# Attention before a mixture of experts: exponentials turned by a product with the diagonal of their inverse sums

## The chip, the core and the metric

The kernel runs on one core of one Trainium2 chip. The metric is the device time of one execution, in microseconds (us). Three runs of the kernel before gave 2071.26, 2071.85 and 2072.37 us; their median is 2071.85.

## What is computed

First comes attention for 4 batches, 8 heads, 768 positions and 64 channels a head, with a mask that keeps the first 8 keys and the last 96 positions. Then a mixture of 8 experts runs on its output of 3072 rows, with weights from eight rounds of alternating normalisation. The attention's share that matters here:

```python
scores = scale * np.matmul(q, k.transpose(0, 1, 3, 2))
...
scores = scores - np.max(scores, axis=-1, keepdims=True)
a = np.exp(scores)
a = a / (np.sum(a, axis=-1, keepdims=True) + 1e-09)
return np.matmul(a, v).astype(np.float32)
```

The division by the sum of a row is what the change moves. A row's sum belongs to a query.

## The kernel before, in words

The class `Banded` does the attention in 32 units of work: a batch, a half of the sequence (3 tiles of 128 queries) and a pair of heads. A unit has three groups, one for each tile of queries, and a group holds both heads. Groups are numbered through as t, from 0 to 95. Because of the mask a tile of queries meets at most 256 keys, so a group has four blocks of 128 keys by 128 queries; the first group of a unit in the first half has two. All units together have 352 blocks.

A group goes through these steps:
- `prepare` (line 309): TensorE turns q and k (tiles `tp`), and ScalarE and VectorE split them into a high and a low part (`qh`, `ql`, `kh`, `kl`).
- `scores` (line 329): three products for each head into PSUM (`s_ps`), for two groups at a time.
- `softmax` (line 352): VectorE adds the bias and finds the row's maximum (line 368, tiles `p_sb` and `mx`); ScalarE takes the exponential and its row sum (line 373, `sm`).
- Behind the third group of a unit, the six sums get EPS (lines 383 and 385), VectorE takes reciprocals (line 386), and a copy spreads each over 64 columns (line 389, tile `inv`).
- `turn` (line 397): TensorE transposes the blocks of exponentials against the identity (line 403, recorded at line 131; from `p_sb` to `t_ps`), and ScalarE or VectorE copies the result to SBUF (line 406, `pT`).
- `invert` (line 494): TensorE transposes the three spread inverses of a unit (`r_ps`), and VectorE copies them back over `inv` (line 500).
- `values` (line 409) and `flush` (line 479): the products of values and turned exponentials (`o_ps`), with channels on the partitions. The two heads write the two halves of the 128 partitions. Then `o_ps` is multiplied by `inv` (line 489), and split into two parts for the experts (lines 490 and 491, tiles `x`).

The order on TensorE is written out by hand. A round does two units, and the tables `FIRST_ROUND` to `ROUND` (lines 58 to 61) say in which order. S is scores and softmax of two groups, T turns two groups, O is `flush`, P is `prepare`, R is `invert` of one unit, and F is filling work for the experts. From the third round on, the rounds start with S, O, S, S. `InOrder` (line 121) keeps TensorE in program order; the order on ScalarE, VectorE and GpSimd is the scheduler's. PSUM tiles of the attention come from one pool of six. `CHUNK` is 2, the number of groups in a step S or T; `P` is 128, `D` is 64, `UT` is 3.

GpSimd works on the experts' weights and inputs meanwhile. Behind the attention the experts fill the rest of the span; there TensorE is busy nearly without a break.

Of the kernel before, what the change touches and what calls it, by code (L numbers as in the profile page):

```python
# [54 lines left out]
BIAS = ((None, (32, 256), (128, 352)), ((0, 384), (32, 256), (128, 352)))  # L55


FIRST_ROUND = (("S", 0), ("O", 0), ("T", 0), ("F", 4), ("P", 0), ("S", 1), ("T", 1), ("F", 4), ("R", 0), ("S", 2), ("R", 1), ("T", 2), ("F", 4), ("P", 1))
SECOND_ROUND = (("S", 0), ("O", 0), ("T", 0), ("F", 4), ("P", 0), ("S", 1), ("T", 1), ("F", 4), ("R", 0), ("R", 1), ("S", 2), ("T", 2), ("F", 4), ("P", 1))
THIRD_ROUND = (("S", 0), ("O", 0), ("S", 1), ("S", 2), ("F", 2), ("T", 0), ("F", 1), ("F", 1), ("T", 1), ("F", 1), ("F", 1), ("P", 0), ("F", 1), ("F", 1), ("T", 2), ("P", 1), ("F", 1), ("R", 0), ("R", 1), ("F", 1), ("F", 1), ("F", 1))  # L60
ROUND = (("S", 0), ("O", 0), ("S", 1), ("S", 2), ("F", 2), ("T", 0), ("F", 1), ("F", 1), ("T", 1), ("F", 1), ("F", 1), ("P", 0), ("F", 1), ("F", 1), ("T", 2), ("F", 1), ("R", 0), ("R", 1), ("F", 1), ("P", 1), ("F", 1), ("F", 1))


class Ordered:
# [69 lines left out]
class Banded:  # L134
# [15 lines left out]
    def __init__(self, tc, q, k, v, early, n_bias):  # L150

        self.tc, self.nc = tc, tc.nc
        self.q, self.k, self.v = q, k, v
        self.H, self.D = q.shape[1], q.shape[3]
        assert n_bias == self.H * self.BIAS1
        self.bias1, rest = early, early[:, n_bias:]
        self.early_q = rest[:, 0:self.Q]
        self.early_k = rest[:, self.Q:self.Q + self.K]
        self.early_v = rest[:, self.Q + self.K:self.Q + self.K + self.V]
        self.d0 = rest[:, self.Q + self.K + self.V:]  # L160
        self.d1 = early[:, n_bias - self.BIAS1:n_bias + self.BIAS1]

        self.early_own = early[:, 5 * self.BIAS1:5 * self.BIAS1 + 2 * P]
        self.second_q = early[:, 4 * self.BIAS1:4 * self.BIAS1 + self.Q]
        self.warm = early[:, 6 * self.BIAS1:6 * self.BIAS1 + 2 * P].bitcast(mybir.dt.bfloat16)
        self.work = [(b, half, g) for b in range(q.shape[0]) for half in range(2) for g in range(self.H // 2)]
        self.pending, self.done, self.begun = [], 0, []
        self.sums, self.inv, self.outs = {}, {}, {}

        self.queue = Ordered(tc, self.nc.sync)  # L170
        self.pe = InOrder(tc)
        self.qs, self.ks, self.vs, self.ready, self.scored = {}, {}, {}, {}, {}
# [179 lines left out]
    def softmax(self, t, s_list):  # L352


        nc, D = self.nc, self.D
        n, group = divmod(t, len(GROUPS))
        _, half, g = self.work[n]
        p_sb = self.wrk.tile([P, 2, 2, P], F32, name="p_sb")
        mx = self.wrk.tile([P, 2], F32, name="mx", bufs=4)
        if group == 0:  # L360
            self.sums[n] = self.wrk.tile([P, UT, 2], F32, name="sm", bufs=4)
        sm = self.sums[n]
        views = []
        for u, (j, i) in enumerate(GROUPS[group]):
            h = 2 * g + j
            pv = p_sb[:, u, 0:len(KEYS[half][i])]
            views.append(pv)
            nc.vector.tensor_tensor_reduce(out=pv, in0=s_list[u], in1=self.bias(h, half, i), scale=-(D ** -0.5), scalar=3.0e38,  # L368
                                           op0=ALU.add, op1=ALU.min, accum_out=mx[:, u:u + 1])
        def exponentials(scalar, us=(0, 1)):  # L370
            for u in us:
                j, i = GROUPS[group][u]
                scalar.activation(out=views[u], in_=views[u], func=AF.Exp, bias=mx[:, u:u + 1], scale=-1.0,  # L373
                                  accum_out=sm[:, i, j:j + 1])

        if t < CHUNK:
            self.begun.append(exponentials)
            return p_sb
        exponentials(nc.scalar)
        if group == len(GROUPS) - 1:  # L380
            begins = n < self.H // 2
            if begins:
                nc.vector.tensor_scalar(out=sm, in0=sm, scalar1=EPS, scalar2=None, op0=ALU.add)
            else:
                nc.scalar.add(sm, sm, EPS)
            nc.vector.reciprocal(out=sm, in_=sm)
            self.inv[n] = self.wrk.tile([P, UT, P], F32, name="inv", bufs=3)
            copy = nc.vector.tensor_copy if n == 0 else nc.scalar.copy if begins else nc.scalar.copy
            copy(out=self.inv[n].rearrange("p t (j d) -> p (t j) d", j=2),
                 in_=sm.rearrange("p t j -> p (t j)").unsqueeze(2).broadcast_to([P, 2 * UT, D]))  # L390
        return p_sb

    def blocks(self, n, group):
        slots = VALUES[self.work[n][1]]
# [1 line left out]

    def turn(self, t):

        p_sb = self.scored.pop(t)
        blocks = self.blocks(*divmod(t, len(GROUPS)))  # L400
        t_ps = self.ps.tile([P, 4, P], F32, name="t_ps", tag="tp")
        for c, (u, a, _, _, _) in enumerate(blocks):
            self.pe.transpose(out=t_ps[:, c], in_=p_sb[:, u, a], identity=self.ident)
        pT = self.wrk.tile([P, 4, P], F32, name="pT", bufs=2 * len(GROUPS))
        copy = self.nc.vector.tensor_copy if t % 2 else self.nc.scalar.copy
        copy(out=pT[:, 0:len(blocks)], in_=t_ps[:, 0:len(blocks)])
        return pT
# [19 lines left out]
    def unit(self, u, xh, xl, between):  # L427

        nc, NG, per = self.nc, len(GROUPS), len(GROUPS) * (self.H // 2)
        if u == 0:
            self.load_k(2)
            self.prepare(0)
            self.own_distances()
            self.scale_bias(0)
            self.keep_warm(self.ps, "tp", WARM0)
            self.ahead(range(0, CHUNK))
            ordered = Ordered(self.tc, nc.scalar)
            self.begun[0](ordered, (0,))  # L440
            self.prepare(1)
            self.load_v(0)
            self.begun[0](ordered, (1,))
            self.begun[1](ordered)
            for g in range(1, self.H // 2):
                self.scale_bias(g)
            for t in range(CHUNK, AHEAD, CHUNK):
                self.ahead(range(t, t + CHUNK))
            self.prepare(2)
            self.load_v(2)  # L450
        for n in range(u * (self.H // 2), (u + 1) * (self.H // 2), 2):
            t, ends = n * NG, n == len(self.work) - 2
            for what, c in FIRST_ROUND if n == 0 else SECOND_ROUND if u == 0 else THIRD_ROUND if n == self.H // 2 else ROUND:
                if what == "S":
                    first = t + (BEHIND if u else AHEAD) + c * CHUNK
                    self.ahead(range(first, first + CHUNK))
                elif what == "O":
                    self.flush()
                elif what == "T":
                    if ends and c == 2:  # L460
                        self.invert(n)
                        self.invert(n + 1)
                        self.flush()
                    for t1 in range(t + c * CHUNK, t + (c + 1) * CHUNK):
                        at = t1 // NG
                        g = at % (self.H // 2)
                        self.pending.append((at, t1 % NG, self.turn(t1), xh[g], xl[g]))
                elif what == "P":
                    self.prepare(n + NG + c)
                    if c == 0 and n + NG == self.H // 2 + 1:  # L470
                        self.load_v(self.H // 2)
                        self.load_k(self.H)
                elif what == "R" and not ends:
                    self.invert(n + c)
                elif what == "F":
                    between(c)
        self.idle = None

    def flush(self):


        for n, group, pT, xh, xl in self.pending:
# [3 lines left out]
            if n % 2 and n != 1:  # L486
                self.load_v(n + 3)
            o_ps = self.outs.pop(n)
            self.nc.vector.tensor_tensor(out=o_ps, in0=o_ps, in1=self.inv.pop(n), op=ALU.mult)
            self.nc.scalar.copy(out=xh, in_=o_ps)  # L490
            self.nc.vector.tensor_tensor(out=xl, in0=o_ps, in1=xh, op=ALU.subtract)
        self.pending = []

    def invert(self, n):

        inv = self.inv[n]
        r_ps = self.turned("r_ps")
        for i in range(UT):
            self.pe.transpose(out=r_ps[:, i], in_=inv[:, i], identity=self.ident)
        self.nc.vector.tensor_copy(inv, r_ps[:, 0:UT])  # L500


class Dense:
# [1466 lines left out]
```

## Time and profile before

| | |
|---|---|
| median of three runs | 2071.85 us |
| the profiled execution's own time | 2070.17 us |
| its span, first to last instruction | 2068.4 us |
| TensorE busy (PE) | 2050.4 us, 99% |
| VectorE (DVE) | 1426.6 us, 69% |
| ScalarE (ACT) | 849.2 us, 41% |
| GpSimd (POOL) | 1553.3 us, 75% |
| granted clock of TensorE, mean | 0.999 |

A busy engine has an instruction in flight. PE is matmul, PEld the load of its stationary side, which runs beside it. A matmul's duration is its whole latency; matmuls overlap, so the time that one costs is the distance from its start to the next one's start. A line number can be a helper's: every recorded matmul of the attention stands at line 128, every recorded transpose at line 131. Names read output<-inputs. The attention takes about the first 250 us of the span.

### The profile page before, as it was taken

The page shows a single profiled execution, that of the slowest core. Times are in us where ns is not written, and L with a number is a line of the kernel's source. Part 1 is how long each engine was busy: PE and PEld are TensorE (multiplying, and loading weights), DVE is VectorE, ACT ScalarE, POOL GpSimd, SP SyncE. Part 2 cuts the span into 40 slices and gives each one's busy share as a digit, 9 for nine tenths or more (in the row PEclk, how much of TensorE's full clock was granted, in tenths as well). Part 3 has the DMA queues.
Part 4 walks back from the last instruction along what each step waited for, and adds up shares of the span by engine and source line. Part 5 has one row for each costly group of instructions (what it writes and reads, how often), then busy time and mean ns, then how long its engine had stood idle before and what let it go on. Part 6 is the DMA issues. An engine that isn't in the chain of part 4 may idle for free.

```text
span 2068.4 us, 30417 instructions
## 1 busy us (share of the span) xinstructions
PE 2050.4 (99%) x10365; PEld 1705.5 (82%) x10365; DVE 1426.6 (69%) x2533; ACT 849.2 (41%) x1783; POOL 1553.3 (75%) x1391
## 2 busy tenths in 40 slices
PE   8999999999999999999999999999999999999998
PEld 6888878888888888788888888888888888888887
DVE  8777787878888888755665565566656565556656
ACT  7787633666656656242222222221322222222221
POOL 6887887788788788677776776777667777677676
PEclk9999999999999999999999999999999999999999
DMA  6787567777787777985665655557966556565553
GB/s 156 213 222 210 164 257 268 279 286 286 277 290 284 269 297 269 376 302 183 204 217 185 205 201 203 199 189 249 338 216 208 187 199 216 187 205 198 204 198 140
DMA packets 229156, 477.48 MB, mean 231 GB/s; under 512 B 107072, under 2 KB 152576, under 8 KB 205696
## 3 DMA queue, kind: packets, MB, share of 16 engines
q1 hardware_dynamic: 228704, 474.40, 67.2%
q8 instruction: 84, 1.38, 0.3%
q0 software_dynamic: 288, 1.05, 0.1%
q14 instruction: 80, 0.66, 0.1%
HBM read 328.75 MB, written 146.64 MB: 230 GB/s over the span
## 4 chain that ended last, share of the span: by engine, by line
PE 58%; DVE 0%; issue 0%
PE c_acc L128 28%; PE bank_a L128 8%; PE bank_c L128 8%; PE bank_d L128 8%; PE bank_b L128 4%; PE o_t L128 2%; DVE early L1692 0%
## 5 line engine op out<-in xcount | busy, mean ns | idle before, releaser
L128 PE MATMUL c_acc<-p,w 128*128 128x512 f32 x2838 | 673.1, 389 | 0.8 <-ACT early L72 0.6
L128 PEld LDWEIGHTS c_acc<-p,w 128*128 128x128 f32 x2838 | 531.7, 188 | 114.2 <-ACT early L72 3.8
L1729 DVE TENSOR_TENSOR early<-early,c_acc 128x512 f32<-128x512 f32 x308 | 210.8, 688 | 180.1 <-PE c_acc L128 180.1
L72 POOL TENSOR_TENSOR early<-raw,full 128x512 f32<-128x512 f32 x56 | 72.8, 1300 | 286.9 <-DVE raw L795 286.9
L128 PE MATMUL bank_d<-x,w 128*128 128x512 f32 x1116 | 283.4, 389 | 0.4 <-DVE xsum L1033 0.4
L128 PE MATMUL bank_a<-m,w 128*128 128x512 f32 x1116 | 283.4, 389 | 0.0
L128 PE MATMUL bank_c<-x,w 128*128 128x512 f32 x1116 | 283.3, 389 | 0.0
L798 ACT CAST p<-raw 128x512 fp32r<-128x512 f32 x150 | 93.1, 621 | 422.9 <-DVE raw L795 333.3
L128 PEld LDWEIGHTS bank_d<-x,w 128*128 128x128 f32 x1116 | 209.4, 188 | 44.2 <-DVE xsum L1033 0.9
L128 PEld LDWEIGHTS bank_c<-x,w 128*128 128x128 f32 x1116 | 209.4, 188 | 43.5
L128 PEld LDWEIGHTS bank_a<-m,w 128*128 128x128 f32 x1116 | 209.4, 188 | 43.5
L72 POOL TENSOR_TENSOR w<-raw,w 128x512 fp32r<-128x512 f32 (+2 forms) x107 | 184.3, 1723 | 57.8 <-ACT w L72 55.8
L72 POOL TENSOR_TENSOR p<-raw,p 128x512 fp32r<-128x512 f32 x151 | 195.2, 1293 | 5.8 <-ACT p L798 5.7
L128 PE MATMUL c_acc<-x,w 128*128 128x512 f32 x774 | 196.5, 389 | 1.2 <-ACT early L72 1.2
L128 PEld LDWEIGHTS c_acc<-x,w 128*128 128x128 f32 x774 | 145.2, 188 | 31.7 <-ACT early L72 1.6
L72 POOL TENSOR_TENSOR p<-full,p 128x512 fp32r<-128x512 f32 x120 | 155.9, 1299 | 3.8 <-ACT p L798 3.8
L806 DVE TENSOR_TENSOR early<-early,bank_d 128x512 f32<-128x512 f32 x63 | 43.3, 688 | 149.8 <-PE bank_d L128 149.7
L128 PE MATMUL bank_b<-m,w 128*128 128x512 f32 x558 | 141.9, 389 | 0.0
L798 ACT CAST p<-full 128x512 fp32r<-128x512 f32 x121 | 75.2, 621 | 160.9 <-POOL full L72 141.0
L128 PEld LDWEIGHTS bank_b<-m,w 128*128 128x128 f32 x558 | 104.7, 188 | 21.7
L373 ACT ACTIVATE p_sb<-p_sb,mx 128x256 f32<-128x256 f32 (+1 forms) x188 | 90.5, 483 | 22.7 <-DVE mx L368 22.1
L804 ACT COPY early<-bank_c 128x512 f32<-128x512 f32 x63 | 37.1, 589 | 150.3 <-PE bank_c L128 150.2
(369 smaller groups left out, 3718.4 us busy)
## 6 DMA issues: line engine op xcount, KB each, us to landing
w<-ws SPq DMA_DIRECT2D x124, 1024.0 KB, 4.9
w<-ws SPq DMA_DIRECT2D x122, 768.0 KB, 4.3
ws<-w SPq DMA_DIRECT2D x54, 1024.0 KB, 5.0
ws<-w SPq DMA_DIRECT2D x53, 768.0 KB, 6.8
raw<-in_moe_w_dram SPq DMA_DIRECT2D x54, 512.0 KB, 5.1
x<-p_rows SPq DMA_DIRECT2D x21, 512.0 KB, 5.2
x<-op_m SPq DMA_DIRECT2D x16, 512.0 KB, 9.9
ws<-w SPq DMA_DIRECT2D x4, 1792.0 KB, 7.1
```

The lines of the kernel that those rows point to most:

```text
L72: return lambda *args, **kw: self.tc.keep_in_program_order(op(*args, **kw))
L128: return self.tc.keep_in_program_order(self.engine.matmul(*args, **kw))
L373: scalar.activation(out=views[u], in_=views[u], func=AF.Exp, bias=mx[:, u:u + 1], scale=-1.0, accum_out=sm[:, i, j:j + 1])
L798: engine.copy(out=ops[k][:, 0], in_=src)
L804: nc.scalar.copy(out=t3, in_=c)
L806: tt(out=t3, in0=t3, in1=d, op=ALU.subtract)
L1729: nc.vector.tensor_tensor(out=sums[k][q], in0=sums[k][q], in1=bank, op=ALU.add)
```

## The change

The sums are now kept for two groups (t and t + 1) instead of for a unit. When both groups have their exponentials, ScalarE adds EPS to the four sums, VectorE takes reciprocals, and VectorE multiplies the identity by each of them, which gives four diagonal matrices of 128 x 128 in one instruction of 128 x 512. `turn` multiplies a block of exponentials by the diagonal of its tile and head, as an ordinary fp32 product, instead of transposing it against the identity. The turned block is thus already divided by the sums. The spread copies, `invert` with its transposes and copies, the R steps of the rounds and the scaling of `o_ps` are dropped.

```diff
-FIRST_ROUND = (("S", 0), ("O", 0), ("T", 0), ("F", 4), ("P", 0), ("S", 1), ("T", 1), ("F", 4), ("R", 0), ("S", 2), ("R", 1), ("T", 2), ("F", 4), ("P", 1))
+FIRST_ROUND = (("S", 0), ("O", 0), ("T", 0), ("F", 4), ("P", 0), ("S", 1), ("T", 1), ("F", 4), ("S", 2), ("T", 2), ("F", 4), ("P", 1))
...
-        if group == 0:
-            self.sums[n] = self.wrk.tile([P, UT, 2], F32, name="sm", bufs=4)
-        sm = self.sums[n]
+        c, at = divmod(t, CHUNK)
+        if at == 0:
+            self.sums[c] = self.wrk.tile([P, CHUNK, 2], F32, name="sm", bufs=4)
+        sm = self.sums[c]
...
         exponentials(nc.scalar)
-        if group == len(GROUPS) - 1:
-            begins = n < self.H // 2
-            if begins:
-                nc.vector.tensor_scalar(out=sm, in0=sm, scalar1=EPS, scalar2=None, op0=ALU.add)
-            else:
-                nc.scalar.add(sm, sm, EPS)
-            nc.vector.reciprocal(out=sm, in_=sm)
-            self.inv[n] = self.wrk.tile([P, UT, P], F32, name="inv", bufs=3)
-            copy = nc.vector.tensor_copy if n == 0 else nc.scalar.copy if begins else nc.scalar.copy
-            copy(out=self.inv[n].rearrange("p t (j d) -> p (t j) d", j=2),
-                 in_=sm.rearrange("p t j -> p (t j)").unsqueeze(2).broadcast_to([P, 2 * UT, D]))
+        if at == CHUNK - 1:
+            self.spread_sums(c)
         return p_sb
+
+    def spread_sums(self, c):
+
+        nc, sm = self.nc, self.sums.pop(c)
+        nc.scalar.add(sm, sm, EPS)
+        nc.vector.reciprocal(out=sm, in_=sm)
+        self.spread[c] = self.wrk.tile([P, CHUNK, 2, P], F32, name="inv", bufs=4)
+        nc.vector.tensor_tensor(out=self.spread[c].rearrange("p c u q -> p (c u) q"),
+                                in0=self.ident.unsqueeze(1).broadcast_to([P, 2 * CHUNK, P]),
+                                in1=sm.rearrange("p c u -> p (c u)").unsqueeze(2).broadcast_to([P, 2 * CHUNK, P]), op=ALU.mult)
...
-        p_sb = self.scored.pop(t)
+        p_sb, inv = self.scored.pop(t), self.spread[t // CHUNK]
...
-            self.pe.transpose(out=t_ps[:, c], in_=p_sb[:, u, a], identity=self.ident)
+            self.pe.matmul(t_ps[:, c], lhsT=p_sb[:, u, a], rhs=inv[:, t % CHUNK, u], start=True, stop=True)
...
-            self.nc.vector.tensor_tensor(out=o_ps, in0=o_ps, in1=self.inv.pop(n), op=ALU.mult)
             self.nc.scalar.copy(out=xh, in_=o_ps)
             self.nc.vector.tensor_tensor(out=xl, in0=o_ps, in1=xh, op=ALU.subtract)
...
-    def invert(self, n):
-
-        inv = self.inv[n]
-        r_ps = self.turned("r_ps")
-        for i in range(UT):
-            self.pe.transpose(out=r_ps[:, i], in_=inv[:, i], identity=self.ident)
-        self.nc.vector.tensor_copy(inv, r_ps[:, 0:UT])
```

The other three tables of rounds lose their R steps in the same way.

On TensorE, in a round of the steady part, the step T of the last two groups with what stands around it. `t_ps` are the turned exponentials, `r_ps` the turned inverses, `tp` q and k, and `y_ps` is filling work. Before:

```order
L128 MATMUL y_ps<-w2h,hh 128x512
L131 MATMUL t_ps<-ident,p_sb 128x128 x8
L131 MATMUL r_ps<-ident,inv 128x128 x6
L128 MATMUL y_ps<-w2l,hh 128x512
L128 MATMUL y_ps<-w2h,hl 128x512
```

And with the change:

```order
L128 MATMUL y_ps<-w2h,hh 128x512
L128 MATMUL t_ps<-inv,p_sb 128x128 x8
L128 MATMUL y_ps<-w2l,hh 128x512
L128 MATMUL y_ps<-w2h,hl 128x512
L131 MATMUL tp<-ident,early 128x128 x3
```

The blocks are turned at the same place, now against `inv`, and the six transposes behind them are gone.

On VectorE, in the same round, behind the last scores. `s_ps1_1193` is the second head's scores of the third S (a score instruction reads as ISA), `pT` the copies of turned blocks, `hl` and `lg` filling work, `ql` and `kl` the low parts of q and k. Before:

```order
L368 ISA p_sb_1212,mx_1213<-s_ps1_1193,early_63 128x256
L368 ISA mx_1213 128x1
L386 RECIPROCAL sm_1111<-sm_1111 128x6
L406 COPY pT_1244<-t_ps_1239 128x512
L1098 COPY lg_134<-gt_ps_1246 128x24
L749 SCALAR_TENSOR_TENSOR hl_1229<-h_ps_1088,hh_1228 128x384
L1099 TENSOR_TENSOR lg_134<-gt_ps_1246,lg_134 128x24
L406 COPY pT_1271<-t_ps_1266 128x512
L386 RECIPROCAL sm_1187<-sm_1187 128x6
L324 TENSOR_TENSOR ql_1277<-tp_1280,qh_1276 128x384
```

And with the change, where the second head's scores of the third S are in `s_ps1_1177`:

```order
L369 ISA p_sb_1200,mx_1201<-s_ps1_1177,early_63 128x256
L369 ISA mx_1201 128x1
L388 RECIPROCAL sm_1103<-sm_1103 128x4
L390 TENSOR_TENSOR inv_1167<-ident_107,sm_1103 128x512
L740 SCALAR_TENSOR_TENSOR hl_1214<-h_ps_1070,hh_1213 128x384
L409 COPY pT_1229<-t_ps_1224 128x512
L1089 COPY lg_134<-gt_ps_1231 128x24
L388 RECIPROCAL sm_1171<-sm_1171 128x4
L1090 TENSOR_TENSOR lg_134<-gt_ps_1231,lg_134 128x24
L390 TENSOR_TENSOR inv_1198<-ident_107,sm_1171 128x512
L409 COPY pT_1256<-t_ps_1251 128x512
L324 TENSOR_TENSOR ql_1262<-tp_1265,qh_1261 128x384
```

`inv_1167` is for the third T of this round, `inv_1198` for the first T of the next; each stands ahead of a copy of turned blocks.

In the first round the diagonals of the first two groups (`inv`) stand on VectorE behind the scores of the next two, `s_ps_350` and `s_ps_351`:

```order
L388 RECIPROCAL sm<-sm 128x4
L369 ISA p_sb,mx<-s_ps_351,early 128x256
L369 ISA mx 128x1
L369 ISA p_sb,mx<-s_ps_350,bias_229 128x128
L369 ISA mx 128x1
L369 ISA p_sb,mx<-s_ps_351,bias_229 128x128
L369 ISA mx 128x1
L390 TENSOR_TENSOR inv<-ident,sm 128x512
```

Before, nothing stood between these exponentials and their turning on VectorE.

## Rows read from the trace of the kernel before

**Rows 1.** The page's busy time, share of the span and instructions of each engine.
```profile
PE 2050.4 (99%) x10365; PEld 1705.5 (82%) x10365; DVE 1426.6 (69%) x2533; ACT 849.2 (41%) x1783; POOL 1553.3 (75%) x1391
```

**Rows 2.** Stages: us, busy PE, PEld, DVE, ACT, POOL, granted clock, DMA share, GB/s.
```profile
10.00:30.00 20.00, 16.78 (x184) 13.95 (x182) 17.82 (x75) 19.24 (x69) 11.82 (x15) 1.00 0.66 148
...
120.00:180.00 60.00, 59.72 (x588) 53.45 (x587) 45.72 (x165) 47.51 (x159) 51.18 (x53) 1.00 0.78 217
```

**Rows 3.** Transposes by tile: count, ns minimum/median/maximum, first and last start.
```profile
L131 PE MATMUL t_ps<-ident,p_sb x352: 270/272/328, 15.1 to 244.2; 128*128 128x128 f32 x176
...
L131 PE MATMUL r_ps<-ident,inv x96: 270/273/330, 19.3 to 241.3; 128*128 128x128 f32 x96
```

**Rows 4.** Timeline of PE at the last T of a round: start, us.
```profile
121.59 1.04 PE L131 MATMUL t_ps<-ident,p_sb 128*128 128x128 f32 x8
122.46 0.82 PE L131 MATMUL r_ps<-ident,inv 128*128 128x128 f32 x6
```

**Rows 5.** Products with values: the group (busy us, mean ns), then PE's timeline.
```profile
L128 PE MATMUL o_ps<-pT,raw_v 128*64 128x128 f32 x352 | 21.2, 275 | 0.0
...
126.15 2.84 PE L128 MATMUL o_ps<-pT,raw_v 128*64 128x128 f32 x48
128.92 0.39 PE L128 MATMUL s_ps<-kl,qh 64*128 64x256 f32 x2
```

**Rows 6.** Tile o_ps from 126.16 to 126.19 us: the records in flight there.
```profile
L128 PE MATMUL o_ps<-pT,raw_v x2: 323/323/323, 126.1 to 126.2; 128*64 128x128 f32 x2
```

**Rows 7.** Short products with 128 columns of weights: group, timeline, load by tile.
```profile
L128 PE MATMUL o_t<-w,x 128*128 128x256 f32 x6 | 1.0, 282 | 0.0
...
2062.62 0.52 PE L128 MATMUL o_t<-w,x 128*128 128x256 f32 x3
...
L128 PEld LDWEIGHTS c_ps<-g_f,ones x16: 186/188/189, 276.8 to 336.2; 128*128 128x128 f32 x16
```

**Rows 8.** Groups that the change drops or multiplies, to 260 us: busy us, mean ns.
```profile
L500 DVE COPY inv<-r_ps 128x384 f32<-128x384 f32 x32 | 16.4, 543 | 0.0
L489 DVE TENSOR_TENSOR o_ps<-o_ps,inv 128x384 f32<-128x384 f32 x32 | 17.8, 561 | 4.6 <-PE o_ps L128 4.4
L386 DVE RECIPROCAL sm<-sm 128x6 f32<-128x6 f32 x32 | 6.0, 186 | 8.0 <-ACT sm L385 7.8
L389 ACT COPY inv<-sm 128x384 f32<-128x384 f32 x31 | 16.0, 515 | 1.0 <-DVE sm L386 0.9
L385 ACT ACTIVATE sm<-sm 128x6 f32<-128x6 f32 x28 | 5.8, 206 | 0.0
```

**Rows 9.** VectorE, two inputs of 128 x 512: one in PSUM, then both in SBUF.
```profile
L324 DVE TENSOR_TENSOR kl<-tp,kh 128x512 fp32r<-128x512 f32 x16 | 11.0, 686 | 0.0
...
L72 DVE TENSOR_TENSOR p<-full,p 128x512 fp32r<-128x512 f32 x39 | 32.6, 835 | 3.2 <-ACT p L72 1.1
L72 DVE TENSOR_TENSOR x<-full,x 128x512 fp32r<-128x512 f32 x12 | 20.1, 1674 | 0.0
```

**Rows 10.** Timeline where exponentials are turned: a steady round, then the first round.
```profile
132.28 0.19 ACT L373 ACTIVATION_READ_ACCUMULATOR p_sb<-p_sb,mx 128x1 f32 x1
...
136.08 1.03 PE L131 MATMUL t_ps<-ident,p_sb 128*128 128x128 f32 x8
...
15.07 0.88 PE L131 MATMUL t_ps<-ident,p_sb 128*128 128x128 f32 x6
...
16.22 0.42 DVE L368 CUSTOM_DVE_ANT_1 p_sb<-s_ps,early 128x256 f32<-128x256 f32 x1
...
17.23 0.31 PEld L131 LDWEIGHTS tp<-ident,raw_k 128*128 128x128 f32 x3 [1.19 <-PE tp L131]
```

**Rows 11.** Waits to 250 us: who for whom, us in total, times, longest.
```profile
PEld tp L131 <- DVE ql L324: 1.8, 3, 0.9
...
PE tp L131 <- DMA early<-in_q_dram: 1.7, 3, 0.6
PEld tp L131 <- DVE pT L406: 1.6, 4, 0.8
```

More of the change, by code (lines that the diff above doesn't have):

```diff
@@ L55 @@
 BIAS = ((None, (32, 256), (128, 352)), ((0, 384), (32, 256), (128, 352)))
-FIRST_ROUND = (("S", 0), ("O", 0), ("T", 0), ("F", 4), ("P", 0), ("S", 1), ("T", 1), ("F", 4), ("R", 0), ("S", 2), ("R", 1), ("T", 2), ("F", 4), ("P", 1))
-SECOND_ROUND = (("S", 0), ("O", 0), ("T", 0), ("F", 4), ("P", 0), ("S", 1), ("T", 1), ("F", 4), ("R", 0), ("R", 1), ("S", 2), ("T", 2), ("F", 4), ("P", 1))
-THIRD_ROUND = (("S", 0), ("O", 0), ("S", 1), ("S", 2), ("F", 2), ("T", 0), ("F", 1), ("F", 1), ("T", 1), ("F", 1), ("F", 1), ("P", 0), ("F", 1), ("F", 1), ("T", 2), ("P", 1), ("F", 1), ("R", 0), ("R", 1), ("F", 1), ("F", 1), ("F", 1))
-ROUND = (("S", 0), ("O", 0), ("S", 1), ("S", 2), ("F", 2), ("T", 0), ("F", 1), ("F", 1), ("T", 1), ("F", 1), ("F", 1), ("P", 0), ("F", 1), ("F", 1), ("T", 2), ("F", 1), ("R", 0), ("R", 1), ("F", 1), ("P", 1), ("F", 1), ("F", 1))
+FIRST_ROUND = (("S", 0), ("O", 0), ("T", 0), ("F", 4), ("P", 0), ("S", 1), ("T", 1), ("F", 4), ("S", 2), ("T", 2), ("F", 4), ("P", 1))
+SECOND_ROUND = (("S", 0), ("O", 0), ("T", 0), ("F", 4), ("P", 0), ("S", 1), ("T", 1), ("F", 4), ("S", 2), ("T", 2), ("F", 4), ("P", 1))
+THIRD_ROUND = (("S", 0), ("O", 0), ("S", 1), ("S", 2), ("F", 2), ("T", 0), ("F", 1), ("F", 1), ("T", 1), ("F", 1), ("F", 1), ("P", 0), ("F", 1), ("F", 1), ("T", 2), ("P", 1), ("F", 1), ("F", 1), ("F", 1), ("F", 1))
+ROUND = (("S", 0), ("O", 0), ("S", 1), ("S", 2), ("F", 2), ("T", 0), ("F", 1), ("F", 1), ("T", 1), ("F", 1), ("F", 1), ("P", 0), ("F", 1), ("F", 1), ("T", 2), ("F", 1), ("F", 1), ("P", 1), ("F", 1), ("F", 1))
 class Ordered:
@@ L167, in __init__ @@
         self.pending, self.done, self.begun = [], 0, []
-        self.sums, self.inv, self.outs = {}, {}, {}
+        self.sums, self.spread, self.outs = {}, {}, {}
         self.queue = Ordered(tc, self.nc.sync)
@@ L371, in exponentials @@
             for u in us:
-                j, i = GROUPS[group][u]
                 scalar.activation(out=views[u], in_=views[u], func=AF.Exp, bias=mx[:, u:u + 1], scale=-1.0,
-                                  accum_out=sm[:, i, j:j + 1])
+                                  accum_out=sm[:, at, u:u + 1])
         if t < CHUNK:
@@ L402, in turn @@
         for c, (u, a, _, _, _) in enumerate(blocks):
-            self.pe.transpose(out=t_ps[:, c], in_=p_sb[:, u, a], identity=self.ident)
+            self.pe.matmul(t_ps[:, c], lhsT=p_sb[:, u, a], rhs=inv[:, t % CHUNK, u], start=True, stop=True)
+        if t % CHUNK == CHUNK - 1:
+            del self.spread[t // CHUNK]
         pT = self.wrk.tile([P, 4, P], F32, name="pT", bufs=2 * len(GROUPS))
@@ L444, in unit @@
             self.begun[1](ordered)
+            self.spread_sums(0)
             for g in range(1, self.H // 2):
@@ L460, in unit @@
                     if ends and c == 2:
-                        self.invert(n)
-                        self.invert(n + 1)
                         self.flush()
@@ L472, in unit @@
                         self.load_k(self.H)
-                elif what == "R" and not ends:
-                    self.invert(n + c)
                 elif what == "F":
```

## The prediction

> **What bounds the kernel now.** I read the busy shares of the page first. TensorE is busy for 2050.4 us of the 2068.4 us span and no other engine is over 75% [rows 1]. The change touches only the attention, so the next view is the table by stage: between 120 and 180 us, where attention rounds alternate with expert work, PE is busy 59.72 of 60 us, DVE 45.72 and ACT 47.51, at a granted clock of 1.00, the 2.4 GHz level [rows 2]. There a nanosecond of PE work is a nanosecond of time, and work taken from DVE or ACT buys nothing by itself. The first rounds differ: from 10 to 30 us PE is busy 16.78 of 20 us, ACT 19.24 and DVE 17.82 [rows 2]; there chains of waits set the pace. So the question is what the change does to PE's time, and second whether PE now waits for something it didn't wait for.
>
> **The transposes that become products.** The 352 turned blocks of exponentials are 352 transposes, one MATMUL record each, of 272 ns median [rows 3]. A record's duration is its latency; the price is the step from one to the next. Eight of them start at 121.59 and the next group at 122.46 [rows 4]: 0.87 / 8 = 0.109 us each.
>
> After the change the stationary side is the same exponentials, the moving side is the scaled diagonal in plain fp32, and it is an ordinary product. The trace has one ordinary fp32 product of that moving width, the one of values with turned exponentials (o_ps). Half of the units read their values from raw_v: 176 blocks, but 352 MATMUL records [rows 5]. An fp32 product is therefore two instructions, and each has the length (275 ns mean) of a whole transpose. In the timeline 48 of them start at 126.15 and the next work at 128.92 [rows 5], 0.058 us each, which looks cheap. But they use 64 columns of the array, and two heads sit side by side: in a 30 ns stretch that only the first two records touch, both are in flight [rows 6]. So each step is 2 x 0.058 = 0.115 us, ends included, and two heads share it. The new products take all 128 columns, so no second one can run beside them: a block costs two full steps.
>
> How long is a step? Lower bound: a transpose's, 0.109, since the record is as long; a block then costs 0.218. Upper bound: the nearest row with the whole array and 128 fresh columns of weights for each short product is o_t at 256 columns: three records take 0.52 us, one lasts 0.282, so a step is (0.52 - 0.282) / 2 = 0.12 [rows 7]; a block then costs 0.240. That the weights may matter is seen in one load of 128 columns for an fp32 product (c_ps): 188 ns, longer than a step [rows 7], and it has to run beside the product before it. I take 0.117 a step, near the upper row because its array use is the same: 0.234 a block.
> - added: 352 x (0.234 - 0.109) = **+44.0 us** (38.4 to 46.1).
>
> The Trainium skill ("FP8 and Floating Point Precision", TensorE Precision Notes) counts a true fp32 product as four passes through the array; two records of double length are four passes, so by that rule the sum would be the 0.218 bound or a little over.
>
> **What falls away on PE.** 96 transposes that turn the inverses [rows 3]; six last 0.82 us and one 0.273 [rows 3, 4], so a step is (0.82 - 0.273) / 5 = 0.109 us: 96 x 0.109 = **-10.5 us**. The order listing of PE shows that nothing else moves in a steady round.
>
> **What falls away and comes on DVE and ACT.** DVE loses 32 copies of 543 ns and 32 scalings of 561 ns; reciprocals go from 32 to 48 at 186 ns. ACT loses 31 copies of 515 ns; additions of EPS go from 28 to 48 at 206 ns [rows 8]. DVE gains 48 products of identity and inverse, 128 x 512 with both inputs in SBUF. With one input in PSUM such an instruction takes 686 ns; with both in SBUF the means are 835 in one group and 1674 in another [rows 9]. So 48 x 0.69 = 33 to 48 x 1.67 = 80 us of DVE; at about 1.0 (nearer to the 835 row, whose other engines are similarly loaded) 48 us. DVE's net is then 48 + 8.9 - 6.0 - 17.4 - 18.0 = +15.5 us over some 230 us: 76% busy becomes 83%. ACT's net is 48 x 0.206 - 28 x 0.206 - 31 x 0.515 = -11.9 us. In the steady rounds both stay below PE, cover: PE's own queue. Priced at nothing.
>
> **The new wait.** A transpose needed only the exponentials. Now it needs the sums of two groups, an addition (ACT), a reciprocal and a product (DVE): 0.21 + 0.19 + 0.69 to 1.67 = 1.1 to 2.1 us, plus their queues. In a steady round the tightest case is the third pair: its exponentials end at 132.47 and PE turns them at 136.08 [rows 10], 3.6 us. The DVE order puts the reciprocal and the product behind eight score instructions and ahead of the copies of turned blocks, so it fits; those copies come a little later, and they are needed only in the next round. PE's own longer products give another 1.5 us a round. Priced at nothing there.
>
> In the first round there is no such slack: PE turned the first pair at 15.07, and the order has DVE finish the next four score instructions first, the last of which starts at 16.22 and lasts 0.42 [rows 10]. The product can end at 17.3 at the earliest, 2.2 us late; PE's queue stood idle for 1.19 us up to 17.23 anyway [rows 10], and DVE is spared a broadcast copy. **+1.5 us** (0 to 4).
>
> **Waits that shrink.** In the attention the transposes of q and k wait three times for a late load of q, 1.7 us in all, and seven times for DVE's ql or its copies of turned blocks, 3.4 us [rows 11]. Rounds longer by 2 us give loads more time, and two PSUM tiles and two DVE copies a pair of units are gone. I take **-3 us** of these 5.1 (0 to -5).
>
> **Sum.** 44.0 - 10.5 + 1.5 - 3 = +32.0 us. The profiled execution took 2070.17 us (span 2068.4), so 2102.2; the median of the runs shown, 2071.85, is 1.7 us above it, so **2103.9**, rounded to 2104. The bounds: 38.4 - 10.5 + 0 - 5 = +22.9 and 46.1 - 10.5 + 4 - 0 = +39.6, from the median 2094.8 to 2111.5.
>
> **Rivals.**
> 1. *The two halves of an fp32 product run at half a step each, faster than before.* If 0.058 us a record held for the full width too, a block would cost 0.115, about a transpose. Then 352 x 0.006 - 10.5 + 1.5 - 3 = -10 us: 2062. It is decided by whether a record at 128 columns steps under 0.07 us. For it: the plain rate in rows 5. Against it: two records in flight at once in rows 6, and the record's length, that of a transpose that steps at 0.109. Chance 0.04.
> 2. *The diagonal is late.* If DVE's product takes 1.7 us and more, DVE nears 97% busy and every pair's turn waits. Half a microsecond at each of 48 pairs adds 24 us: 2128. It decides from the point where reciprocal and product end 3.6 us after the last exponential. For it: the 1674 ns row, and POOL busy 75% [rows 1, 9]. Against it: the slack in rows 10 and the 83%. Chance 0.07.
> 3. *PE's extra is swallowed.* If the first eight units, with 88 of the blocks, took their 88 x 0.109 = 9.6 us beside their waits, and the pauses went wholly, with steps of 0.109, the sum would be 38.4 - 9.6 - 10.5 + 1.5 - 5 = +14.8: 2087. For it: the first rounds in rows 2. Against it: their PE is 84% busy too, and later there is hardly idle time. Chance 0.06.
> 4. *A plain fp32 product is four times a transpose.* Four steps of 0.109, 0.436 a block, would be 352 x 0.327 - 10.5 = +104.6 us: 2176. The Trainium skill ("TensorE: Matmul & The Clock Gate", Terms) calls the transpose mode four times faster for fp32. Against it: rows 5 show two records a block, not four, each no longer than a transpose. Chance 0.02.
>
> **How the numbers follow.** The forecast has 0.81; with it the range 2094 to 2112, its own bounds, leaves out rivals 1, 2, 4 and most of 3. About 0.2% (4 us) is what a measurement of this kernel tells from no change: under 2067.7 lies rival 1, 0.04; within 4 us a mixture of rivals 1 and 3, 0.02; the rest, 0.94, is slower.
>
> **What would show it.** In the profile after: 704 MATMUL records of t_ps with 128 columns, some 270 to 280 ns long, groups of eight that take 1.75 to 1.95 us instead of 0.87; no r_ps; the end of the attention some 30 us later and the stages behind it as long as before. PE's idle time in 60 to 250 us should not grow by more than a few microseconds; if it waits there for DVE's inv, rival 2 has part of it. A group of eight in about 0.9 us, or in 3.5, would make the price of the product wrong; a DVE product far over 1.0 us would make DVE's net wrong.

## The result and the profile after

The changed kernel took 2093.95 us (median of four runs, 2093.36 to 2094.75), the kernel before 2071.72 beside it: 22.2 us slower, a ratio of 1.0107 (1.0090 to 1.0125). The forecast was 2104, 32 us slower, and its range began at 2094, just above the measured time. The direction was right, the size too large by 10 us.

The page's busy time of the kernel after, which answers to [rows 1]:

```profile
PE 2076.4 (99%) x10621; PEld 1736.9 (83%) x10621; DVE 1433.5 (69%) x2528; ACT 840.6 (40%) x1772; POOL 1569.4 (75%) x1391
```

TensorE has 256 records more: 352 second halves of products, less 96 transposes of inverses. Its stages, with the columns of [rows 2]:

```profile
10.00:30.00 20.00, 17.62 (x190) 15.57 (x187) 17.34 (x71) 17.93 (x69) 12.07 (x15) 1.00 0.66 149
120.00:180.00 60.00, 60.00 (x592) 55.71 (x589) 44.70 (x155) 42.61 (x149) 47.68 (x43) 1.00 0.71 195
```

In the steady stage PE has no idle time left (60.00 of 60 us, 59.72 before), and DVE is busy 75% of it, not the 83% that I had worked out. Where the attention ends, from the tile view of `o_ps` (count, ns minimum/median/maximum, first and last start), before:

```profile
L128 PE MATMUL o_ps<-pT,raw_v x352: 272/273/323, 35.4 to 246.6; 128*64 128x128 f32 x176
```

and after:

```profile
L128 PE MATMUL o_ps<-pT,raw_v x352: 272/273/323, 37.0 to 268.6; 128*64 128x128 f32 x176
```

The last of these products starts 22.0 us later, and the spans of these two profiled executions differ by 23.3 us (2091.7 against 2068.4). So all but 1.3 us of the difference arises in the attention. Behind that start the profiled executions of the ten kernels shown here take between 1819.7 and 1824.9 us, so 1.3 us there says nothing of the change.

The price of a turned block, first from the tile view of `t_ps`, then from PE's timeline around one step T (start, us):

```profile
L128 PEld LDWEIGHTS t_ps<-inv,p_sb x704: 186/192/192, 15.4 to 266.1; 128*128 128x128 f32 x176
L128 PE MATMUL t_ps<-inv,p_sb x704: 271/275/377, 15.4 to 266.2; 128*128 128x128 f32 x176
...
131.69 1.95 PE L128 MATMUL t_ps<-inv,p_sb 128*128 128x128 f32 x16
133.39 0.47 PE L128 MATMUL y_ps<-w2l,hh 128*128 128x512 f32 x1
133.71 0.39 PE L128 MATMUL y_ps<-w2h,hl 128*128 128x512 f32 x1
```

There are two records a block. Sixteen of them last 1.95 us and one 0.275, so a step is (1.95 - 0.275) / 15 = 0.112 us, and a block costs 0.224, between the bounds of 0.218 and 0.240. The added term was thus 352 x (0.224 - 0.109) = 40.5 us, not 44.0. With the 96 transposes gone (10.5 us) the attention issues 30.0 us more PE work, and 22.2 us of it became time. **About 8 us are missing**, where the prediction had taken 3.

What PE waits for up to 272 us (us in total, times, longest), all that this view lists, which answers to [rows 11]:

```profile
PE s_ps L128 <- DVE kl L324: 1.7, 2, 1.1
PE w_ps L128 <- DVE early L1917: 1.4, 1, 1.4
PE t_ps L128 <- DVE inv L390: 1.3, 3, 0.6
PE t_ps L128 <- DVE x L490: 0.9, 1, 0.9
PE tp L131 <- POOL early L221: 0.5, 1, 0.5
```

The three waits of `tp` for q's load are gone, and PEld's list of the same stretch has no wait of `tp` for `ql` or the copies of turned blocks. The new wait for the diagonals (`inv`) is 1.3 us. Counted by rounds, from the start of the fifth round's step O to that of the attention's last flush, first before, then after:

```profile
65.20:245.80 180.60, 178.44 (x1756) 159.68 (x1754) 135.61 (x475) 140.24 (x461) 155.50 (x178) 1.00 0.71 196
```

```profile
70.00:267.80 197.80, 197.80 (x1950) 183.50 (x1948) 143.09 (x473) 133.66 (x450) 164.51 (x174) 1.00 0.65 180
```

The stretch grew by 17.2 us. It holds 264 blocks and 72 transposes of inverses, so the steps say 264 x 0.115 - 72 x 0.109 = 22.5. Here 5.3 us vanished, yet only 2.2 us of idle PE were there to vanish (180.60 - 178.44). Up to the fifth round's step O, behind the first eight units, the growth was 4.8 us (70.0 - 65.2), where 88 x 0.115 - 24 x 0.109 = 7.5 were added; another 2.7 vanished.

The rest of the idle time is hidden. PE's timeline of the kernel before, twice around filling work:

```profile
137.78 0.34 PE L128 MATMUL h_ps<-x,w1l 128*128 128x384 f32 x1
137.96 0.33 PE L128 MATMUL h_ps<-x,w1h 128*128 128x384 f32 x1
138.43 1.26 PE L131 MATMUL tp<-ident,early 128*128 128x128 f32 x7
...
152.91 0.50 PE L128 MATMUL y_ps<-w2l,hh 128*128 128x512 f32 x1
153.50 0.50 PE L128 MATMUL y_ps<-w2h,hl 128*128 128x512 f32 x1
```

and DVE's, where the input of the last one is made:

```profile
152.89 0.56 DVE L749 SCALAR_TENSOR_TENSOR hl<-h_ps,hh 128x384 fp32r<-128x384 f32 x1
```

The two `y_ps` products start 0.59 us apart, because `hl` ends at 153.45; in the kernel after they start 0.32 apart (133.39 and 133.71 above). So 0.27 us is lost, and only 0.09 of it lies outside a record (152.91 + 0.50 to 153.50). At 137.96 the step to the next start is 0.47 where the one before it was 0.18, with 0.14 outside a record; and the seven transposes last 1.26 us, where six steps of 0.109 and one record of 0.273 make 0.93. In-flight records cover most of each pause, so neither the busy share nor the waits show its size. The Trainium skill ("Perfetto Trace Analysis", Identifying the Most-Contended Engine) calls matmul busy time a poor measure of how close a kernel is to its limit, because matmuls are pipelined. These rows agree, with 2.2 us of visible idle time beside 5.3 that vanished.

### The profile page after: what moved, and what is told of

The parts are those of the page before. It is cut to its first block, busy times and chain, and to the rows that moved or that the text cites. A ratio compares the mean times of both kernels' runs of the same rounds, so it can differ in the third digit from the quotient of the medians.

```text
span 2091.7 us, 30813 instructions
## 1 busy us (share of the span) xinstructions
PE 2076.4 (99%) x10621; PEld 1736.9 (83%) x10621; DVE 1433.5 (69%) x2528; ACT 840.6 (40%) x1772; POOL 1569.4 (75%) x1391
## 4 chain that ended last, share of the span: by engine, by line
PE 90%; DVE 5%; ACT 2%; POOL 1%; issue 1%; DMA 0%; DVEq 0%; SPq 0%; ACTq 0%; POOLq 0%
PE c_acc L128 36%; PE bank_d L128 11%; PE bank_a L128 11%; PE bank_c L128 11%; PE bank_b L128 6%; PE y_ps L128 4%; PE t_ps L128 3%; PE o_ps L128 2%; PE o_t L128 2%; PE s_ps L128 2%; PE h_ps L128 1%; DVE early L72 1%; PE tp L131 1%; DVE p L72 1%; DVE full L72 1%
```

## The experiments

**Theory.** The kernel before loses 8 to 10 us to short PE waits in the attention (q's loads, `hl`, copies), mostly hidden under records; anything that makes the steps T longer covers them, whoever does it. **Rivals.** The product costs less on average than its timeline step; or the diagonals on DVE cost or save time themselves; or the dropped work on DVE and ACT was worth something.

**The product alone, the work alone, and the diagonals alone.** Three kernels take the change apart. The first is the kernel before, with products against the plain identity:

```diff
-            self.pe.transpose(out=t_ps[:, c], in_=p_sb[:, u, a], identity=self.ident)
+            self.pe.matmul(t_ps[:, c], lhsT=p_sb[:, u, a], rhs=self.ident, start=True, stop=True)
```

> The kernel before, with one edit: the exponentials are turned by an fp32 product with the identity instead of a transpose; the inverses, their transposes, copies and the scaling all stay. Both theories price the product at two steps of 0.112 us a block, 352 x 0.115 = +40.5 us. Theory A (the missing 8 us are waits that vanish because PE's own steps are longer, whatever else is done): +32 to +34, 2104 to 2106 us. Theory B (they vanish because the inverses' transposes, PSUM tiles and copies are gone): +40, 2111 to 2113 us.

Measured: 2100.68 us, 29.05 over before (ratio 1.0144, 1.0127 to 1.0161). That is 3 us under theory A's range and far from theory B's. The steps added 40.5; 11.4 vanished although neither DVE's nor ACT's work was changed.

The second is the kernel before without inverses, R steps and scaling:

```diff
-        if group == len(GROUPS) - 1:
...
-                    self.invert(n + c)
+                    pass
...
-            self.nc.vector.tensor_tensor(out=o_ps, in0=o_ps, in1=self.inv.pop(n), op=ALU.mult)
```

> The kernel before without the inverses: no addition of EPS, reciprocal, spread, transposes, copies, and no scaling, so the attention's output is not divided by its sums. The exponentials are transposed as before. PE loses 96 x 0.109 = 10.5 us. Theory A (waits vanish only with longer steps): -10 to -5, 2061 to 2067 us, the waits for q and for the filling work's low parts stay or grow. Theory B (relief): -10.5 and most of the 8 us of waits, 2053 to 2056 us.

Measured: 2066.52 us (2063.89 to 2069.21), 5.1 under before (0.9978, 0.9968 to 0.9987). PE was spared 10.5 us, and half came through, at the small end of theory A. PE's waits of this kernel begin with q's load, which had 1.7 us before:

```profile
PE tp L131 <- DMA early<-in_q_dram: 6.0, 5, 2.7
PE tp L131 <- DVE kl L324: 2.8, 2, 1.9
```

So the slack runs both ways: shorter rounds run into the loads. The longest of these waits is in PE's timeline, with the idle time before it in brackets, and the stages behind it follow:

```profile
75.08 0.33 PE L128 MATMUL h_ps<-x,w1h 128*128 128x384 f32 x1
78.11 1.30 PE L131 MATMUL tp<-ident,early 128*128 128x128 f32 x5 [2.69 <-DMA early<-in_q_dram]
```

```profile
78.50:81.90 3.40, 3.40 (x20) 2.96 (x20) 1.25 (x2) 1.07 (x2) 3.32 (x4) 0.50 0.77 209
81.90:85.30 3.40, 3.40 (x42) 3.17 (x40) 1.30 (x9) 2.35 (x9) 3.24 (x3) 0.63 0.99 315
85.30:90.00 4.70, 4.70 (x51) 4.37 (x48) 4.17 (x19) 3.26 (x12) 4.54 (x5) 1.00 0.62 166
```

After 2.69 us without work the granted clock was 0.50, the 1.2 GHz level, and then back at 1.00. At these clocks the stages gave away about 3.40 x 0.50 + 3.40 x 0.37 = 3.0 us. With the pause that is 5.7, about what is missing in this execution (10.5 - 5.1 = 5.4).

The third is the changed kernel, with transposes again; the diagonals are made, and no one reads them:

```diff
-            self.pe.matmul(t_ps[:, c], lhsT=p_sb[:, u, a], rhs=inv[:, t % CHUNK, u], start=True, stop=True)
+            self.pe.transpose(out=t_ps[:, c], in_=p_sb[:, u, a], identity=self.ident)
```

> The changed kernel with one edit: the exponentials are transposed against the identity again, and the diagonals are made but not read, so the output is not divided by its sums. Theory A: 2094 - 40.5 + 8, 2060 to 2066 us, a little above the kernel without inverses at most. Theory B: 2094 - 40.5, 2053 to 2056 us.

Measured: 2082.37 us, 10.7 over before (1.0046, 1.0029 to 1.0064), and 15.9 over the kernel without inverses, from which it differs by the 48 reciprocals, additions and diagonals alone. That is outside both expected ranges: DVE's work, costed at nothing, costs 16 us where T is short. PEld's waits up to 262 us show where:

```profile
PEld y_ps L128 <- DVE hl L740: 9.4, 6, 1.7
PEld s_ps L128 <- DVE kl L324: 7.2, 8, 2.1
...
PEld y_ps L128 <- ACT hh L739: 3.8, 6, 0.8
```

and DVE's timeline at one such wait shows how:

```profile
95.78 1.23 DVE L390 TENSOR_TENSOR inv<-ident,sm 128x512 f32<-128x512 f32 x1
96.94 0.55 DVE L324 TENSOR_TENSOR ql<-tp,qh 128x384 fp32r<-128x384 f32 x1
97.41 0.68 DVE L324 TENSOR_TENSOR kl<-tp,kh 128x512 fp32r<-128x512 f32 x1
98.00 0.54 DVE L740 SCALAR_TENSOR_TENSOR hl<-h_ps,hh 128x384 fp32r<-128x384 f32 x1
```

A diagonal of 1.23 us stands ahead of `ql`, `kl` and `hl`, and PE's next product needs that `hl`, at 98.54. DVE is not overloaded; its order makes filling work late. The stage from 120 to 180 us has DVE busy 46.76 of 60 us, and a granted clock below 1.00:

```profile
120.00:180.00 60.00, 55.40 (x505) 48.35 (x502) 46.76 (x154) 42.65 (x150) 47.84 (x44) 0.97 0.70 194
```

In the four stages of 60 us up to 240 us the granted clock is 0.97, 0.94, 0.97 and 0.97, in the kernel without inverses 1.00, 0.94, 1.00 and 1.00. By these shares about 9.0 us are lost here against 3.6 there. So some 5 of the 16 us are, by this estimate, what the clock lost behind the waits, and the rest is the waits.

**The diagonals in the changed kernel.** If they cost 16 us there too, the product's own price would be far lower than its steps say. So they were left out of the changed kernel, with the plain identity in their place:

```diff
-        if at == CHUNK - 1:
-            self.spread_sums(c)
...
-            self.pe.matmul(t_ps[:, c], lhsT=p_sb[:, u, a], rhs=inv[:, t % CHUNK, u], start=True, stop=True)
+            self.pe.matmul(t_ps[:, c], lhsT=p_sb[:, u, a], rhs=self.ident, start=True, stop=True)
```

> The changed kernel with fp32 products against the identity; no addition, reciprocal or diagonal is made, so the output is not divided by its sums. PE does the same work as the changed kernel, VectorE loses 48 x 0.71 + 48 x 0.19 = 43 us. Theory A (under the long T steps VectorE's diagonals are covered): within 2 us of the changed kernel, 2092 to 2095 us. If the diagonals still hold up PE there: 2085 to 2090 us.

Measured: 2093.94 us (1.0108, 1.0091 to 1.0125): the time of the changed kernel, within theory A's range. Under the long products the diagonals cost nothing that the medians can show (their intervals leave some 3.5 us). In the profiled execution the last `o_ps` starts 1.0 us earlier than in the changed kernel (267.6 against 268.6), about what PE waited there for `inv`. And made twice:

```diff
+        for _ in range(2):
+            nc.vector.tensor_tensor(out=self.spread[c].rearrange("p c u q -> p (c u) q"),
...
```

> The changed kernel with every product that makes the diagonals issued twice: VectorE gains 48 x 0.71 = 34 us in the attention, PE's work is the same. Theory A with cover left: 2094 to 2098 us. If the cover is used up already (transposes in place of the products cost 11 us less than the products although they save 40 us of PE, so some 29 us of VectorE's lateness lie under the T steps): 2104 to 2120 us.

Measured: 2118.71 us, 48.0 over before (1.0225, 1.0208 to 1.0242), 24.8 over the changed kernel. The cover is used up by the first set. The group of the diagonals (us busy, mean ns), then PE's first waits up to 290 us:

```profile
L391 DVE TENSOR_TENSOR inv<-ident,sm 128x512 f32<-128x512 f32 x96 | 97.3, 1014 | 1.7
```

```profile
PE y_ps L128 <- DVE hl L741: 6.9, 4, 2.5
PE t_ps L128 <- DVE inv L391: 5.3, 5, 1.8
PE s_ps L128 <- DVE kl L324: 4.5, 5, 2.0
```

This is rival 2 of the prediction, brought about: a late diagonal, and late filling work beside it.

**Longer steps T of a known price.** The missing 8 us could still be a product that is cheaper than its step. The test needs no product: in the kernel before, every block is transposed twice into the same place, at 0.109 us a step, or only those of every second group (`range(1 + t % 2)`).

```diff
-            self.pe.transpose(out=t_ps[:, c], in_=p_sb[:, u, a], identity=self.ident)
+            for _ in range(2):
+                self.pe.transpose(out=t_ps[:, c], in_=p_sb[:, u, a], identity=self.ident)
```

> The kernel before with every transpose of exponentials issued twice onto the same place: PE gains 352 x 0.109 = 38.4 us in the same T steps, nothing else is edited. Theory A (some 8 to 11 us of waits in the attention vanish when the T steps are longer, whatever makes them longer): +27 to +31, 2099 to 2103 us. Rival (only the fp32 product gives time back, or only the inverses' removal does): +37 to +39, 2109 to 2111 us.

> As the one above for the odd groups alone, 176 blocks: PE gains 19.2 us. Theory A, if the waits are short ones of under a microsecond that a little more PE time already covers: +9 to +13, 2081 to 2085 us. If they need the whole length: +15 to +17. Rival: +19, 2090 to 2092 us.

Measured: 2099.01 us with all (28.3 over before; 1.0133, 1.0116 to 1.0150) and 2081.25 with half (10.5 over; 1.0049, 1.0032 to 1.0066), both in theory A's ranges. The steady stage with all transposed twice shows PE full:

```profile
120.00:180.00 60.00, 60.00 (x612) 55.19 (x611) 43.57 (x156) 42.30 (x141) 41.56 (x39) 1.00 0.69 190
```

Where the attention ends in the runs with half transposed twice, with all, and with the product with the identity:

```profile
L128 PE MATMUL o_ps<-pT,raw_v x352: 272/273/323, 36.3 to 258.3; 128*64 128x128 f32 x176
L128 PE MATMUL o_ps<-pT,raw_v x352: 272/273/323, 37.8 to 276.0; 128*64 128x128 f32 x176
L128 PE MATMUL o_ps<-pT,raw_v x352: 272/273/324, 38.0 to 277.9; 128*64 128x128 f32 x176
```

Together, by the medians and by the last start of `o_ps` in the profiled execution (246.6 us before):

| kernel | PE work added, us | median over before | last `o_ps` over before | missing by median, by last start |
|---|---|---|---|---|
| half transposed twice | 176 x 0.109 = 19.2 | 10.5 | 11.7 | 8.7, 7.5 |
| all transposed twice | 352 x 0.109 = 38.4 | 28.3 | 29.4 | 10.1, 9.0 |
| product with identity | 352 x 0.115 = 40.5 | 29.05 | 31.3 | 11.4, 9.2 |
| the change | 40.5 - 10.5 = 30.0 | 22.2 | 22.0 | 7.8, 8.0 |

The intervals leave each median some 3.5 us, so the medians don't tell the rows apart. They do show that all four miss at least 2.5 times the forecast's 3 us. Two of the rows have transposes alone, at a known step, so a cheaper product falls as the cause. Doubling the added work from 19.2 to 38.4 us raises what is missing by only 1.4 or 1.5: what vanishes is a stock of waits, not a share of the work.

The traces also show where the stock lay. I added up PE's steps from one start to the next, up to the last start of `o_ps`, each counted for the record that it leads to. This is the part of the work that no edit touches, with the same count of records in every kernel (us, worked out from the starts in the traces):

| kernel | q and k (`tp`) | scores (`s_ps`) | filling `y_ps` | filling `h_ps` | together |
|---|---|---|---|---|---|
| before | 31.4 | 45.5 | 25.8 | 28.4 | 131.1 |
| half transposed twice | 27.1 | 44.5 | 24.1 | 28.4 | 124.0 |
| all transposed twice | 26.6 | 44.4 | 24.1 | 28.4 | 123.5 |
| product with identity | 27.2 | 44.4 | 24.2 | 28.5 | 124.3 |
| the change | 26.1 | 44.1 | 24.2 | 28.5 | 122.8 |

The same instructions take 6.8 to 8.3 us less in all four, and 4.2 to 5.3 of that was waiting ahead of the transposes of q and k. What made T longer did not matter.

**Another way to divide.** With transposes back, DVE could multiply the exponentials in place by the inverse sums, which needs neither diagonals nor R:

```diff
+        for at in range(CHUNK):
...
+            nc.vector.tensor_tensor(out=pv, in0=pv, in1=sm[:, at].unsqueeze(2).broadcast_to([P, 2, w]), op=ALU.mult)
```

> A candidate: as the changed kernel, but VectorE multiplies the exponentials in place by the inverse of their row's sum (the row is the partition there), 96 products of 128 x 512 instead of 48, and TensorE transposes them against the identity. PE then has neither the inverses' transposes nor the fp32 products. VectorE gains 48 x 0.71 = 34 us over the changed kernel, some 89% busy in the attention. Theory A: 2060 to 2067 us. Theory B: 2053 to 2058 us. If VectorE becomes the bound or the scaled exponentials are late: 2072 us and more.

Measured: 2120.96 us, 49.3 over before (1.0240, 1.0222 to 1.0257), the last of the expected cases. The 80 products of 128 x 512 on DVE (16 more have 256 columns), then PE's first waits and the stage from 60 to 120 us:

```profile
L394 DVE TENSOR_TENSOR p_sb<-p_sb,sm 128x512 f32<-128x512 f32 x80 | 81.9, 1056 | 1.0
```

```profile
PE y_ps L128 <- DVE hl L740: 14.7, 5, 3.9
PE t_ps L131 <- DVE p_sb L394: 11.3, 11, 3.5
```

```profile
60.00:120.00 60.00, 47.88 (x380) 40.66 (x378) 49.61 (x127) 31.30 (x107) 49.43 (x43) 0.86 0.63 176
```

Now PE idles a fifth of the stage, and its granted clock falls with it. No run here that divides beat the kernel before; even without any division the gain was 5 us.

## Why the prediction was right and wrong

- **The transposes that become products**: right in kind (two records a block, no pairing of heads, a step near a transpose's), and 3.5 us too dear: 0.112 a step where I took 0.117, inside the bounds. A load of 192 ns hides beside the product before it; the row of `o_t` (0.12) was not the nearer end.
- **What falls away on PE**: the 96 transposes went, 10.5 us of work.
- **What falls away and comes on DVE and ACT**: priced at nothing, and the diagonals cost next to nothing in this kernel, as the run without them shows. But the reason given, that both engines stay below PE in the steady rounds, was not enough: the run with transposes has the same DVE load and pays 16 us for it. The cover was the longer T, and it is used up. The diagonals took 849 ns in the mean, against the 1000 taken. Their tile view:

```profile
L390 DVE TENSOR_TENSOR inv<-ident,sm x48: 676/706/2010, 14.6 to 258.6; 128x512 f32<-128x512 f32 x48
```

The median is near the 686 ns with one input in PSUM, and single ones reach 2010. The Trainium skill ("SBUF — State Buffer", Who interferes with whom) says that a DVE instruction with two SBUF inputs contends with a GpSimd instruction that reads SBUF; the traces agree. In the changed kernel, the one with transposes again and the one with diagonals twice, 7, 8 and 18 diagonals ran with no GpSimd instruction beside them, and these took 675 to 695 ns. Every one over 700 ns had one beside it. This is the longest, with GpSimd's:

```profile
39.39 2.01 DVE L390 TENSOR_TENSOR inv<-ident,sm 128x512 f32<-128x512 f32 x1
38.47 2.38 POOL L656 TENSOR_TENSOR w1l<-w1f,w1h 128x1024 fp32r<-128x1024 f32 x1
```
- **The new wait**: 1.5 us taken for the first round. PE's timeline of the kernel after:

```profile
15.38 1.38 PE L128 MATMUL t_ps<-inv,p_sb 128*128 128x128 f32 x10 [0.25 <-DVE inv L390]
```

It began 0.3 us later than the first transposes before [rows 3], not 2.2. The prediction had taken the wrong score instructions. The last of the four that stand ahead of the diagonal is one of 128 x 128 with `bias`, while the one at 16.22 us [rows 10] is 128 x 256 with `early` and belongs to the next step S. Here is DVE at that place, first before, then after:

```profile
14.38 0.28 DVE L368 CUSTOM_DVE_ANT_0 p_sb<-s_ps,bias 128x128 f32<-128x128 f32 x1
```

```profile
14.43 0.29 DVE L369 CUSTOM_DVE_ANT_0 p_sb<-s_ps,bias 128x128 f32<-128x128 f32 x1
14.64 0.69 DVE L390 TENSOR_TENSOR inv<-ident,sm 128x512 f32<-128x512 f32 x1
```

So the 1.3 us measured, close to the 1.5 taken, is luck: it is made of three waits of the first round (0.25, 0.58 and 0.44 us), one for each pair of groups, and not of one for the first pair. In the steady rounds there was no wait worth counting, as said.
- **Waits that shrink**: **this is the step that failed.** It took 3 us, with 5 as its bound, because it added up the waits that the wait view names for q, `ql` and copies [rows 11]. What vanished was about 8 us, and up to 9 or 11 with longer T. The view names a wait only by the time that no record covers; in the pair of `y_ps` shown above 0.18 of the 0.27 us lost lay under a record. The premise that in the steady rounds a nanosecond of PE work is a nanosecond of time fell with it. With the measured terms the sum is 40.5 - 10.5 - 8 = 22.0, against 22.2 measured. The 8 is what is left over in this sum; the table of steps finds 8.3 us less in front of the unchanged work, from the starts alone. The first round's wait is inside the 8.
- **The rivals**: a product at half a step (1) and at four steps (4) fell with 0.112 and two records. The late diagonal (2) did not decide here, but it was one more set of diagonals away. The swallowed extra (3) was the right mechanism in the wrong place: it put 9.6 us into the first eight units, where 2.7 vanished; the other 5.3 came out of rounds that the busy share called full.

Left open: of the 5.3 us ahead of q's and k's transposes, how much each of q's loads, `kl`, `ql` and the copies of turned blocks held. A further buffer for q, or a DVE order that keeps `hl` ahead of reciprocals and diagonals, would tell; neither was tried.

## What to carry to other kernels

A TensorE that reads 99% busy can still hold a stock of short waits: compare starts of the same pair of instructions in different rounds, and when a change adds PE work, expect that stock to be used up before the clock on the wall moves one for one; when it removes PE work, expect waits to come back. Here work put on another engine was hidden or not by its place in that engine's order, not by the engine's load, so look for what stands behind it and who waits for that. In fp32 a full-width product is not a cheap transpose: here it cost 0.224 us a block instead of 0.109, 40.5 us in all, where leaving out the transposes, copies and scalings that it replaced was worth 5.1.

## What the hardware showed

- A full-width fp32 product of 128 columns steps at 0.112 us a record although each load of its stationary side is shown as 192 ns. The Trainium skill ("TensorE: Matmul & The Clock Gate", Terms) gives fp32 four times the speed in transpose mode; the blocks here say 0.224 / 0.109 = 2.05, and the measurement decides.
- A pause of 2.69 us in which PE waited for one load was followed by 3.40 us at a granted clock of 0.50 and 3.40 at 0.63, so the wait cost about twice its length.
- DVE's product of 128 x 512 with both inputs in SBUF had no one price: 675 to 695 ns with no GpSimd instruction beside it, up to 2010 in the changed kernel with one. The mean was 849 ns for the 48 diagonals of the changed kernel, 977 for the same 48 with transposes again, 1014 for 96, and 1056 for 80 scalings of exponentials.
